# A third late q chunk, Wp in the freed accumulation banks, a scheduler with small waits and perturbed passes, and 12 warm matmuls instead of 16, in a two-pair linear-attention and FFN kernel

## The chip, the cores and the metric

The kernel runs on one core of one Trainium2 chip. Times are device microseconds of a run; the number quoted for a kernel is the median of its runs. A run's *span* is the time from its first to its last instruction. Every run has the granted TensorE clock in its records (1.0 is full speed).

## The reference, cut to what matters

```python
# x: (1, 2048, 512) bf16; wqkv: (512, 1536); wo: (512, 512); w1: (512, 1376); w2: (1376, 512)
phi = lambda t: jnp.where(t > 0, t + 1, jnp.exp(t)) + 1e-6
def A(x):                      # linear attention, 32 heads of 16
    q, k, v = heads(x @ wqkv)
    kv  = einsum("bhsd,bhse->bhde", phi(k), v)       # a sum over all 2048 rows
    z   = einsum("bhsd->bhd", phi(k))
    num = einsum("bhqd,bhde->bhqe", phi(q), kv)
    den = einsum("bhqd,bhd->bhq", phi(q), z) + 1e-6
    return merge(num / den) @ wo
def B(x): return relu(x @ w1) @ w2
x = x + A(layernorm(x));  x = x + B(layernorm(x))
x = x + A(layernorm(x));  x = x + B(layernorm(x))
```

No output of an attention layer can be computed before the sums `kv` and `z` over all rows are done. That is the *barrier* of this document; there are two.

## The kernel before

The kernel is a graph of operations, each with an engine, a modelled duration, and what it reads and writes. A list scheduler in the kernel's own Python orders the operations of each engine when the kernel is built; the order is then fixed, and each engine runs its list in order, waiting on semaphores. The 2048 rows are 16 tiles, or 4 chunks of 4 tiles. `k`, `gacc` (accumulation for kv, in four PSUM banks `GB` that stay taken), `z`, `q`, `den`/`denb` (denominator and its reciprocal, spread over the heads), `u` (scaling of q), `wp` (kv times wo), `wo` (output projection), `h` and `ffo` (the two halves of the FFN) are its steps.

```python
# scheduler, forward pass, for each engine e:
            st0 = min(c[0] for c in cands)
            lim = st0 + SLACK[e]                     # SLACK is 0 everywhere before
            st, o = min((c for c in cands if c[0] <= lim), key=lambda c: (-c[1].prio, c[1].idx))
...
# each q or k group: two evictions on ScalarE, two operations on VectorE
g.add(ACT, ... activation(dst_ap, psv[:, b, :], Identity, bias=1.0 + 1e-6) ..., name="_lin")
g.add(ACT, ... activation(escr[:, s, :], psv[:, b, :], Exp) ...,            name="_exp")
g.add(DVE, ... tensor_scalar(emscr[:, s, :], escr[:, s, :], 1.0, 1e-6, min, add) ..., name="_em")
g.add(DVE, ... tensor_tensor(dst_ap, dst_ap, emscr[:, s, :], max) ...,      name="_phi")
...
def bar():                                           # the barrier, in program order
    late = list(range(max(0, NCH - Q_LATE), NCH))    # Q_LATE = 2: chunks 2 and 3
    for i in range(NT - LAG, NT): a_g_acc(i, GB)
    ... a_z_acc ...; a_z_final(zb); a_g_evac(GB)
    for t in late[:LATE_A]: a_q_proj(t, late=True)
    a_kv()
    for t in range(DEN_PRE): a_den(t, GB)
    for t in late[LATE_A:]: a_q_proj(t, late=True)
    a_wp()
...
def a_wp():
    for j in range(4):
        b = alloc_bank()                             # any free PSUM bank
        mm_group(... KVT[:, j, :], wo[:, j, :] ... -> bank b); evac_flex(Wp[:, j, :] <- bank b)
...
# denominator of chunk t: four matmuls, then ScalarE Ln and Exp(-), VectorE rhi and rsp,
# four matmuls into the GB banks, four VectorE multiplications "u"
```

A `q` chunk that isn't late is computed in the projection phase, between the k groups. A layer norm's output reaches TensorE by DMA transposes, two tiles each (the first chunk's by TensorE).

## Time and profile before

| | before |
|---|---|
| time, median of the first 3 runs | 295.24 us |
| span of the profiled run | 293.0 us |
| TensorE busy, by the page | 282.9 us (97%) |
| VectorE, ScalarE busy | 164.0 us (56%), 171.8 us (59%) |
| first useful TensorE instruction | 7.18 us |
| last matmul starts | 290.04 us |

The page's part 1, engine: busy us (share of the span) and instructions:

```profile
PE 282.9 (97%) x1470; PEld 129.3 (44%) x1491; DVE 164.0 (56%) x485; ACT 171.8 (59%) x349; POOL 20.7 (7%) x32
```

97% doesn't mean that 3% is all there is to win or to lose: the Trainium skill says ("Perfetto Trace Analysis", Per-engine timelines) that a matmul's end is computed, not observed, and this trace gives matmuls of 379 ns mean that start 216 ns apart. So I count what TensorE *lost* from start times: the step from one matmul's start to the next, less what that shape takes in an unbroken stream (128x512: 0.216 us; 128x256: 0.109; 128x128: 0.056; one column: 0.026; a group of four tiled denominator matmuls: 0.318). The page has 1491 weight loads and only 1470 matmuls: some matmul records are missing, so a surplus of just one more 0.216 us is taken for a missing record. (Where the clock is at half, this count is blind: each matmul then looks like a missing record.) Sums of these steps:

| stretch | lost before |
|---|---|
| start: until the first useful instruction, and steps up to 36 us | 7.18 + 1.39 = 8.57 us |
| first barrier and the FFN beside it, 36 to 86 us | 2.89 us |
| 86 to 155 us | 0.19 us |
| second barrier, 174 to 228 us | 2.99 us |

About 0.6 us of the first barrier's sum are six steps of 0.1 us around the tiled groups. The rest sits at three steps around the Wp matmuls (0.52, 0.24, 0.26 us) and one that looks like 1.50 us. The view of TensorE's waits for 36 to 86 us (line waited for: us, times, longest), then the timeline (start us, us, engine, line, op, out<-in, count, idle before):

```profile
PE ps L573 <- DVE emscr L557: 1.4, 1, 1.4
PE ps L573 <- DVE Wp L652: 0.4, 1, 0.4
```

```profile
58.54 2.61 SPq L522 DMA_TRANSPOSE Tb<-xn  x2
...
59.53 2.47 DVE L720 TENSOR_TENSOR big<-big,ps 128x512 bf16<-128x512 bf16 x4
...
60.47 0.40 PE L573 MATMUL ps<-big,Zc 128*32 128x512 bf16 x4
...
62.06 2.27 PEld L573 LDWEIGHTS ps<-Wp,big 128*128 128x128 bf16 x12 [1.49 <-DVE big L720]
62.29 2.54 PE L573 MATMUL ps<-Wp,big 128*128 128x512 bf16 x11 [1.43 <-DVE emscr L557]
```

At 60.8 us TensorE has run out of late q groups. The next in its list is chunk 1's output projection (`ps<-Wp,big`), which needs the four scalings (`big<-big,ps`) that end at 62.0; its weight loads name them as what they waited for. Chunk 0's transposes were issued at 58.54 and land at 63.82 and 64.60, so no FFN matmul is ready either. And in the view of windows (busy us and count of PE, PEld, DVE, ACT, POOL; clock; DMA) VectorE and ScalarE have no room here:

```profile
54.00:64.00 10.00, 8.57 (x45) 3.55 (x44) 10.00 (x31) 9.67 (x23) 0.00 (x0) 1.00 0.54 54
```

### The profile page before, as it was taken

How to read it: one execution, taken by the hardware profiler on the slowest of the kernel's cores; microseconds unless marked ns; L12 is line 12 of the kernel's file. 1: busy time of each engine (PE TensorE's matmuls, PEld its weight loads, DVE VectorE, ACT ScalarE, POOL GpSimd, SP SyncE). 2: the span in 40 equal slices, each digit the busy share in tenths (PEclk: the TensorE clock that was granted, in tenths of full speed). 3: DMA queues.
4: the chain of work that ended last, by engine and by line, in shares of the span. 5: the costliest groups of instructions: out<-in, count | busy, mean ns of one | idle time of the engine just before them, and what ended most of it. 6: DMA issues, size and time to landing. Idle time of an engine off the chain costs nothing.

```text
span 293.0 us, 4025 instructions
## 1 busy us (share of the span) xinstructions
PE 282.9 (97%) x1470; PEld 129.3 (44%) x1491; DVE 164.0 (56%) x485; ACT 171.8 (59%) x349; POOL 20.7 (7%) x32
## 2 busy tenths in 40 slices
PE   7999999989999999999999999998999999999996
PEld 2444445434444444444444444533444444444443
DVE  5998637996349551480326474599832955130233
ACT  1888757997664583597623486599766407317000
POOL 4213000002001110010001100000100011000000
PEclk9999999999999999999999999999999999999999
DMA  6945930073003070030000340004610424001022
GB/s 224 346 78 104 303 122 2 0 75 61 10 2 72 0 143 2 1 72 0 3 0 0 72 74 0 2 0 73 39 36 0 34 71 112 0 11 63 0 72 74
DMA packets 40163, 17.23 MB, mean 59 GB/s; under 512 B 31984, under 2 KB 39632, under 8 KB 40144
## 3 DMA queue, kind: packets, MB, share of 16 engines
q1 hardware_dynamic: 40144, 16.98, 26.7%
q8 instruction: 12, 0.20, 0.3%
q14 instruction: 7, 0.06, 0.1%
HBM read 7.01 MB, written 2.10 MB: 31 GB/s over the span
## 4 chain that ended last, share of the span: by engine, by line
PE 83%; DVE 11%; DMA 3%; issue 1%; SPq 0%
PE ps L573 83%; DVE big L720 3%; DMA xin<-in_A_x_dram 2%; DVE xres L586 2%; DMA Tb<-xn 1%; DVE big L559 1%; DVE Wp L652 1%; DVE bst L483 1%; DVE emscr L557 1%; DVE xn L593 1%; DVE rsp L714 1%; DVE rhi L713 0%; DVE xn L515 0%; DVE nmf L589 0%; DVE xin L760 0%
## 5 line engine op out<-in xcount | busy, mean ns | idle before, releaser
L573 PE MATMUL ps<-Tb,w 128*128 128x512 bf16 (+1 forms) x352 | 78.0, 379 | 0.0
L573 PE MATMUL ps<-w,big 128*128 128x512 bf16 (+3 forms) x355 | 76.4, 372 | 0.4
L741 ACT ACTIVATE big<-ps 128x512 bf16<-128x512 f32 (+1 forms) x81 | 48.2, 596 | 29.4 <-PE ps L573 28.9
L580 ACT ACTIVATE sqscr<-xres 128x512 bf16<-128x512 f32 x48 | 30.3, 635 | 42.7 <-DVE xres L617 27.9
L573 PEld LDWEIGHTS ps<-w,big 128*128 128x128 bf16 (+1 forms) x363 | 35.4, 98 | 40.8
L573 PEld LDWEIGHTS ps<-Tb,w 128*128 128x128 bf16 (+1 forms) x352 | 34.9, 100 | 40.9 <-issue 0.9
L555 ACT ACTIVATE escr<-ps 128x512 bf16<-128x512 f32 x64 | 38.4, 613 | 9.7 <-PE ps L573 9.7
L553 ACT ACTIVATE big<-ps 128x512 bf16<-128x512 f32 x64 | 38.3, 613 | 3.0 <-PE ps L573 3.0
L613 DVE SCALAR_TENSOR_TENSOR xin<-ps,rstdf,xres 128x512 bf16<-128x512 f32 x15 | 11.3, 750 | 38.5 <-PE ps L573 38.5
L573 PE MATMUL ps<-wqkv,Tb 128*128 128x512 bf16 x125 | 31.4, 379 | 0.3
L573 PE MATMUL ps<-Wp,big 128*128 128x512 bf16 x124 | 28.7, 379 | 3.0 <-DVE emscr L557 2.9
L573 PE MATMUL ps<-big,xn 128*128 128x512 bf16 x124 | 31.3, 379 | 0.2
L573 PE MATMUL ps<-Tb,wqkv 128*128 128x512 bf16 x128 | 30.5, 380 | 0.1
L557 DVE TENSOR_SCALAR emscr<-escr 128x512 bf16<-128x512 bf16 x64 | 17.8, 290 | 21.7 <-ACT escr L555 21.2
L559 DVE TENSOR_TENSOR big<-big,emscr 128x512 bf16<-128x512 bf16 x64 | 26.0, 422 | 3.9 <-ACT big L553 3.5
L617 DVE SCALAR_TENSOR_TENSOR xres<-ps,rstdf,xres 128x512 f32<-128x512 f32 x16 | 12.0, 751 | 24.8 <-PE ps L573 24.8
L720 DVE TENSOR_TENSOR big<-big,ps 128x512 bf16<-128x512 bf16 x32 | 20.1, 681 | 7.9 <-PE ps L573 7.9
L573 PEld LDWEIGHTS ps<-Wp,big 128*128 128x128 bf16 x128 | 12.2, 98 | 17.6 <-DVE big L720 3.0
L573 PEld LDWEIGHTS ps<-big,xn 128*128 128x128 bf16 x128 | 12.5, 98 | 15.1 <-DVE big L559 0.2
L573 PEld LDWEIGHTS ps<-wqkv,Tb 128*128 128x128 bf16 x128 | 12.2, 98 | 15.2 <-DMA Tb<-xn 0.6
L573 PEld LDWEIGHTS ps<-Tb,wqkv 128*128 128x128 bf16 x128 | 11.7, 98 | 15.3 <-issue 1.8
L606 POOL TENSOR_TENSOR rstdf<-varf,nhalf 128x4 f32<-128x4 f32 x8 | 8.1, 1007 | 144.6 <-DVE varf L604 144.6
(76 smaller groups left out, 180.7 us busy)
## 6 DMA issues: line engine op xcount, KB each, us to landing
wqkv<-in_A_wqkv_dram SPq DMA_DIRECT2D x3, 512.0 KB, 6.9
xin<-in_A_x_dram SPq DMA_DIRECT2D x3, 512.0 KB, 7.9
out_dram<-xin SPq DMA_DIRECT2D x3, 512.0 KB, 2.9
w<-in_B_w_dram SPq DMA_DIRECT2D x1, 1376.0 KB, 6.3
w<-in_B_w_dram SPq DMA_DIRECT2D x1, 1280.0 KB, 9.8
wo<-in_A_wo_dram SPq DMA_DIRECT2D x1, 512.0 KB, 8.6
Tb<-xn SPq DMA_TRANSPOSE x30, 3.2
xin<-in_A_x_dram SPq DMA_DIRECT2D x1, 384.0 KB, 3.3
```

Source lines behind the costliest of these rows:

```text
L553: g.add(ACT, lambda e: e.activation(dst_ap, psv[:, b, :], ACTF.Identity, bias=1.0 + 1e-6, scale=1.0), [("ps", b)], [dst_key], C_ACT_PSUM, ...
L555: g.add(ACT, lambda e: e.activation(escr[:, s, :], psv[:, b, :], ACTF.Exp), [("ps", b)], [("escr", s)], C_ACT_EXP, name=name + "_exp")
L557: g.add(DVE, lambda e: e.tensor_scalar(emscr[:, s, :], escr[:, s, :], 1.0, 1e-6, ALU.min, ALU.add), [("escr", s)], [("emscr", s)], C_DVE_B ...
L559: g.add(DVE, lambda e: e.tensor_tensor(dst_ap, dst_ap, emscr[:, s, :], ALU.max), [dst_key, ("emscr", s)], [dst_key], 340.0, name=name + "_ ...
L573: last = e.matmul(o, l, r, start=st, stop=sp, skip_group_check=skip)
L580: g.add(ACT, lambda e: e.activation(sqscr[:, q, :], xres[:, i, :], ACTF.Square, accum_out=dst[:, i:i + 1]), [("xres", i)], [("sqscr", q), ...
L586: g.add(DVE, lambda e: e.scalar_tensor_tensor(xres[:, i, :], psv[:, b, :], 0.0, src, ALU.add, ALU.add, accum_out=s1f[:, i:i + 1]), [("ps", ...
L606: g.add(POOL, lambda e: e.tensor_tensor(rstdf[:, sl], varf[:, sl], nhalf[:, 0:4], ALU.pow), [("varf", t), ("nhalf",)], [("rstdf", t)], C_P ...
L613: g.add(DVE, lambda e: e.scalar_tensor_tensor(xin[:, i, :], psv[:, b, :], rstdf[:, i:i + 1], xres[:, i, :], ALU.mult, ALU.add), rd, [("xin ...
L617: g.add(DVE, lambda e: e.scalar_tensor_tensor(xres[:, i, :], psv[:, b, :], rstdf[:, i:i + 1], xres[:, i, :], ALU.mult, ALU.add, accum_out= ...
L720: g.add(DVE, lambda e, j=j: e.tensor_tensor(unit_ap(us[j]), unit_ap(us[j]), psv[:, GB[j], :], ALU.mult), [("big", us[j]), ("ps", GB[j])], ...
L741: g.add_flex([(ACT, lambda e, M=M, b=b, u=u: e.activation(unit_ap(u, M), psv[0:M, b, :], ACTF.Relu), C_ACT_PSUM), (DVE, lambda e, M=M, b=b ...
```

## The change

Its intent is to give TensorE other work across the barrier, to take bank waits out of it, and to let the scheduler pass over an operation that is ready for a more urgent one that comes within a small wait. The core of the diff:

```diff
-SLACK = {PE: 0.0, ACT: 0.0, DVE: 0.0, POOL: 0.0, SP: 0.0}
+SLACK = {PE: 60.0, ACT: 100.0, DVE: 150.0, POOL: 0.0, SP: 0.0}
 # modelled costs: C_DVE_STT 615 -> 630, C_DVE_NORM_BF 325 -> 330, transposes 470 + 740 a tile ->
 # 1270 + 550 a tile, DMA latency 1500 -> 1600, one-column matmul 30 -> 26
@@ def _list_schedule
-    for _ in range(iters):                       # 6 passes, best total kept
+    for k in range(iters):                       # 12 passes, best score kept
         _backward(ops, succ, rank)
+        ...
+        sigma = rng.choice((0.0, 0.0, 200.0, 600.0, 2000.0)) if k >= 4 else 0.0
         for o in ops:
-            rank[o.idx] = o.t_start
+            rank[o.idx] = src[4][o.idx][3] + rng.gauss(0.0, sigma)
+    for _ in range(search):                      # search is 0
+        ...
-def build_kernel(..., Q_LATE=2, ..., WARM=16, ..., ITERS=6):
+def build_kernel(..., Q_LATE=3, ..., WARM=12, ..., WP_GB=True, ..., ITERS=12, SEARCH=0, ...):
@@
-        def a_wp():
+        def a_wp(GB):
             for j in range(4):
-                b = alloc_bank()
+                b = GB[j] if WP_GB else alloc_bank()
```

Cut: options that stay off (row sums on GpSimd, statistics on ScalarE, a load from ScalarE's queue), and the activation table load, which moves behind leading DMA issues of ScalarE's queue (there are none).

More of the change, by code (lines that the diff above doesn't have):

```diff
@@ L1 @@
 import contextlib
-import math
+import random
 import concourse.bass as bass
@@ L24 @@
 C_DVE_PSUM = 600.0
-C_DVE_STT = 615.0
+C_DVE_STT = 630.0
+C_DVE_STTP = 690.0
 C_DVE_BF4X = 205.0
@@ L28 @@
 C_DVE_BNST = 595.0
-C_DVE_NORM_BF = 325.0
+C_DVE_NORM_BF = 330.0
 C_POOL_POW = 1000.0
@@ L38 @@
 C_SP_ISSUE = 470.0
+C_SP_TR = 1270.0
+C_MMN1 = 26.0
 TAIL = {PE: 70.0, ACT: 230.0, DVE: 80.0, POOL: 300.0, SP: 0.0}
 SYNC_LAT = 40.0
-SLACK = {PE: 0.0, ACT: 0.0, DVE: 0.0, POOL: 0.0, SP: 0.0}
+SLACK = {PE: 60.0, ACT: 100.0, DVE: 150.0, POOL: 0.0, SP: 0.0}
 class _Op:
     __slots__ = ("eng", "emit", "reads", "writes", "dur", "lat", "sdeps", "odeps", "idx",
-                 "seq", "dma", "name", "t_start", "t_done", "t_ready", "issued", "prio", "alts")
+                 "seq", "dma", "name", "t_start", "t_done", "t_ready", "issued", "prio", "alts", "force", "cls")
     def __init__(self, eng, emit, reads, writes, dur, lat, dma, name):
@@ L59, in __init__ @@
         self.alts = None
+        self.force = None
+        self.cls = name.rstrip("0123456789_")
         self.seq = None
@@ L218, in _forward @@
                 st = max(t, fa)
-                if o.alts:
+                if o.force is not None:
+                    if o.force != e:
+                        continue
+                elif o.alts:
                     mine = [d for (x, _, d) in o.alts if x == e][0]
@@ L263, in _forward @@
         if o.dma:
-            dma_free = max(st + 1500.0, dma_free) + o.lat
+            dma_free = max(st + 1600.0, dma_free) + o.lat
             o.t_done = dma_free + 500.0
@@ L280, in _forward, with _list_schedule, score, run @@
     return total, order, vbank, bank_after, snap
-def _list_schedule(ops, tile_ops, vbank, fixed_sp, iters=6, nbanks=8):
+def _list_schedule(ops, tile_ops, vbank, fixed_sp, iters=6, search=0, nbanks=8):
     succ = _succs(ops)
+    npe = float(sum(1 for o in ops if o.eng == PE))
+    def score(res):
+        return res[0] + 0.05 * sum(v[3] for v in res[4].values() if v[0] == PE) / npe
+    def run():
+        for o in ops:
+            o.prio = base[o.idx] + bias[o.idx]
+        try:
+            return _forward(ops, succ, tile_ops, nbanks, fixed_sp)
+        except RuntimeError:
+            return None
+    rng = random.Random(7)
     rank = {o.idx: float(o.idx) for o in ops}
-    best = None
-    for _ in range(iters):
+    bias = [0.0] * len(ops)
+    best = best_base = None
+    for k in range(iters):
         _backward(ops, succ, rank)
-        res = _forward(ops, succ, tile_ops, nbanks, fixed_sp)
-        if best is None or res[0] < best[0]:
+        base = [o.prio for o in ops]
+        res = run()
+        if res is not None and (best is None or score(res) < score(best)):
+            best, best_base = res, base
+        src = res if res is not None and k % 8 != 7 else best
+        sigma = rng.choice((0.0, 0.0, 200.0, 600.0, 2000.0)) if k >= 4 else 0.0
+        for o in ops:
+            rank[o.idx] = src[4][o.idx][3] + rng.gauss(0.0, sigma)
+    base = best_base
+    for _ in range(search):
+        old_bias = list(bias)
+        snap = best[4]
+        c = rng.choice(ops)
+        t0 = snap[c.idx][3]
+        w = rng.choice((2000.0, 6000.0, 15000.0))
+        sd = rng.choice((100.0, 400.0, 1500.0))
+        for o in ops:
+            if abs(snap[o.idx][3] - t0) <= w:
+                bias[o.idx] += rng.gauss(0.0, sd)
+        res = run()
+        if res is not None and score(res) <= score(best):
             best = res
-        for o in ops:
-            rank[o.idx] = o.t_start
+        else:
+            bias = old_bias
     total, order, vb, bank_after, snap = best
@@ L306, in _list_schedule, with build_kernel @@
     return order, total
-def build_kernel(nc, A_x, A_wqkv, A_wo, B_w1, B_w2, out, n_layers_pairs=2, Q_LATE=2, O_PE_CHUNKS=3, PHI_PATH=3,
-                 KV_LAG=2, INTERLEAVE=True, WARM=16, SPLIT_CHUNKS=1, TAIL_SPLIT=True,
+def build_kernel(nc, A_x, A_wqkv, A_wo, B_w1, B_w2, out, n_layers_pairs=2, Q_LATE=3, O_PE_CHUNKS=3, PHI_PATH=3,
+                 KV_LAG=2, INTERLEAVE=True, WARM=12, SPLIT_CHUNKS=1, TAIL_SPLIT=True,
                  PHI_K=3, PHI_QE=3, PHI_QL=3, LAST_HALVES=True, ZH_FIRST=True, P2_TIGHT=False,
-                 FIRST_PE_CHUNKS=1, TGK=2, TGF=2, WO_LAG=1, DEN_PRE=1, LATE_A=1, ITERS=6):
+                 FIRST_PE_CHUNKS=1, TGK=2, TGF=2, FT_PE=0, WP_GB=True, WO_LAG=1, DEN_PRE=1, LATE_A=1, ITERS=12, SEARCH=0, ZP=0, WK_ACT=False, ACT_STATS=()):
     S = A_x.shape[1]
@@ L375, in build_kernel @@
         Zc = sb("Zc", [128, 4, 32], BF16)
+        zacc = sb("zacc", [128, 512], F32)
+        zhl = sb("zhl", [128, 2, 512], BF16)
         GT = sb("GT", [128, 4, 512], BF16)
@@ L404, in build_kernel, with dma @@
         scr_state = {"e": 0, "sq": 0, "ln": 0}
-        def dma(emit, reads, writes, xfer_ns, name):
+        def dma(emit, reads, writes, xfer_ns, name, eng=SP, issue=C_SP_ISSUE):
             sem = es.enter_context(nc.semaphore("dsem%d" % len(dma_sems)))
@@ L411, in _emit @@
                 return emit(eng).then_inc(sem, 16)
-            op = g.add(SP, _emit, reads, writes, dur=C_SP_ISSUE, lat=xfer_ns, dma=True, name=name)
+            op = g.add(eng, _emit, reads, writes, dur=issue, lat=xfer_ns, dma=True, name=name)
             op.seq = sem
@@ L439, in build_kernel @@
         ld_x(0, 1)
-        dma(lambda e: e.dma_start(wqkv[:, :, D:2 * D], wq_v[:, :, D:2 * D]), [], [("wk",)], 1600.0, "ld_wk")
+        dma(lambda e: e.dma_start(wqkv[:, :, D:2 * D], wq_v[:, :, D:2 * D]), [], [("wk",)], 1600.0, "ld_wk", eng=ACT if WK_ACT else SP)
         for t in range(1, NCH):
@@ L446, in build_kernel @@
         dma(lambda e: e.dma_start(wo[:], A_wo.rearrange("(c p) n -> p c n", p=128)), [], [("wo",)], 1600.0, "ld_wo")
-        early_loads = list(g.ops)
+        early_loads = [o for o in g.ops if o.eng == SP]
         nfull = NFC - 1 if FLAST < 128 else NFC
@@ L453, in build_kernel @@
             dma(lambda e: e.dma_start(w2[0:FLAST, NFC - 1, :], B_w2[nfull * 128:DFF, :]), [], [("w2b",)], 600.0, "ld_w2b")
-        late_loads = g.ops[len(early_loads):]
+        late_loads = [o for o in g.ops if o.eng == SP][len(early_loads):]
         W2KEYS = [("w2a",), ("w2b",)] if FLAST < 128 else [("w2a",)]
@@ L523, in tr_dma @@
                                                 xn[:, lo:hi, :].rearrange("p i d -> p (i d)")),
-                [("xn", i) for i in range(lo, hi)], [("T", i) for i in range(lo, hi)], 740.0 * (hi - lo), "tr%d" % lo)
+                [("xn", i) for i in range(lo, hi)], [("T", i) for i in range(lo, hi)], 550.0 * (hi - lo), "tr%d" % lo, issue=C_SP_TR)
         def tr_chunk(t, grain):
@@ L626, in a_k_proj @@
             phi_evac(b, pk_tile(i), ("big", pk_unit(i)), "k%d" % i, path=PHI_K)
+            if 0 < i < 4 * ZP:
+                prev = pk_tile(0) if i == 1 else zacc[:, :]
+                pkey = ("big", pk_unit(0)) if i == 1 else ("zacc",)
+                g.add(POOL, lambda e: e.tensor_tensor(zacc[:, :], prev, pk_tile(i), ALU.add),
+                      [("big", pk_unit(i)), pkey], [("zacc",)], C_POOL_TT, name="zp%d" % i)
+                if i == 4 * ZP - 1:
+                    g.add(POOL, lambda e: e.tensor_copy(zhl[:, 0, :], zacc[:, :]), [("zacc",)], [("zhl", 0)], C_POOL_CP, name="zhi")
+                    g.add(POOL, lambda e: e.tensor_tensor(zhl[:, 1, :], zacc[:, :], zhl[:, 0, :], ALU.subtract),
+                          [("zacc",), ("zhl", 0)], [("zhl", 1)], C_POOL_TT, name="zlo")
         def a_g_acc(i, GB):
@@ L632, in a_g_acc, with a_z_acc, src @@
                      [("big", u), ("xn", i)], [("ps", b) for b in GB], 4 * C_MM512, "gacc%d" % i)
-        def a_z_acc(lo, hi, zb):
-            def mk():
-                mms = []
-                for i in range(lo, hi):
-                    u = pk_unit(i)
-                    for j in range(4):
-                        mms.append((psv[:, zb, j:j + 1], big[:, u * 512 + 128 * j:u * 512 + 128 * j + 128], ones[:, 0:1],
-                                    i == 0 and j == 0, i == NT - 1, True))
-                return mms
-            mm_group(mk, [("big", pk_unit(i)) for i in range(lo, hi)] + [("ones",)], [("ps", zb)], (hi - lo) * 4 * C_MMTINY, "z%d" % lo)
+        def a_z_acc(lo, hi, zb, first):
+            def src(i, j):
+                if i < 0:
+                    return zhl[:, i + 2, 128 * j:128 * j + 128]
+                u = pk_unit(i)
+                return big[:, u * 512 + 128 * j:u * 512 + 128 * j + 128]
+            def mk():
+                return [(psv[:, zb, j:j + 1], src(i, j), ones[:, 0:1], first and i == lo and j == 0, i == NT - 1, True)
+                        for i in range(lo, hi) for j in range(4)]
+            mm_group(mk, [("zhl", i + 2) if i < 0 else ("big", pk_unit(i)) for i in range(lo, hi)] + [("ones",)], [("ps", zb)],
+                     (hi - lo) * 4 * C_MMN1, "z%d" % lo)
         def a_z_final(zb):
@@ L798, in ln_tile_first @@
         def ln_tile_first(i):
-            ln_stats_first(i)
             c = slice(i, i + 1)
+            if i in ACT_STATS:
+                g.add(ACT, lambda e: e.activation(sqscr[:, 0, :], xin[:, i, :], ACTF.Identity, accum_out=s1[:, c]),
+                      [("xin", i)], [("sqscr", 0), ("s1", i)], C_ACT_SQ, name="sm%d" % i)
+                g.add(ACT, lambda e: e.activation(sqscr[:, 1, :], xin[:, i, :], ACTF.Square, accum_out=s2[:, c]),
+                      [("xin", i)], [("sqscr", 1), ("s2", i)], C_ACT_SQ, name="sq%d" % i)
+                g.add(DVE, lambda e: e.tensor_scalar(mv[:, i, 0:1], s1[:, c], INV_D, None, ALU.mult),
+                      [("s1", i)], [("mean", i)], C_DVE_SMALL, name="mean%d" % i)
+                g.add(DVE, lambda e: e.scalar_tensor_tensor(nm2[:, c], mv[:, i, 0:1], -1.0, mv[:, i, 0:1], ALU.mult, ALU.mult),
+                      [("mean", i)], [("nm2", i)], C_DVE_SMALL, name="nm2_%d" % i)
+                g.add(DVE, lambda e: e.scalar_tensor_tensor(mv[:, i, 1:2], s2[:, c], INV_D, nm2[:, c], ALU.mult, ALU.add),
+                      [("s2", i), ("nm2", i)], [("var", i)], C_DVE_SMALL, name="var%d" % i)
+            else:
+                ln_stats_first(i)
             g.add(DVE, lambda e: e.tensor_scalar(veps[:, c], mv[:, i, 1:2], 0.0, EPS, ALU.max, ALU.add),
@@ L864, in bar @@
                     zb = alloc_bank()
-                    for k in range(NCH):
-                        a_z_acc(4 * k, 4 * k + 4, zb)
+                    if ZP:
+                        a_z_acc(-2, 0, zb, True)
+                    for k in range(ZP, NCH):
+                        a_z_acc(4 * k, 4 * k + 4, zb, k == 0)
                     a_z_final(zb)
@@ L875, in bar @@
                         a_q_proj(t, late=True)
-                    a_wp()
+                    a_wp(GB)
                 def p2(t):
@@ L883, in p2 @@
                             a_wo(i, first_layer)
-                        tr_chunk(t - WO_LAG, TGF)
+                        if t - WO_LAG < FT_PE:
+                            for i in range(4 * (t - WO_LAG), 4 * (t - WO_LAG) + 4):
+                                transpose_pe(i)
+                        else:
+                            tr_chunk(t - WO_LAG, TGF)
                         ln_ffn(t - WO_LAG)
@@ L924, in build_kernel @@
             cur = nxt
-        order, total = _list_schedule(g.ops, g.tile_ops, vbank, early_loads + first_tr + late_loads, ITERS)
+        order, total = _list_schedule(g.ops, g.tile_ops, vbank, early_loads + first_tr + late_loads, ITERS, SEARCH)
         for e in (PE, ACT, DVE, POOL):
-            for k, o in enumerate(order[e]):
+            for k, o in enumerate([o for o in order[e] if not o.dma]):
                 o.seq = k + 1
@@ L958, in emit_engine @@
         def emit_engine(e, handle):
+            lead = True
             for o in order[e]:
+                if e == ACT and lead and not o.dma:
+                    lead = False
+                    handle.preload_act_table_set("natural_log_exp_and_others")
                 for d in waits[o.idx]:
@@ L978, in _ @@
             def _(s):
-                s.preload_act_table_set("natural_log_exp_and_others")
                 emit_engine(ACT, s)
```

## The prediction

> **What bounds the kernel now.** The page gives TensorE 282.9 of 293.0 us busy (97%). The Trainium skill ("Perfetto Trace Analysis", Per-engine timelines) says that matmul ends are estimated, so I go by start-to-start times. In the timeline a 128x512 matmul starts 0.216 us after the one before it; the skill's 215.7 ns ("TensorE: Matmul & The Clock Gate", Part 1) agrees. Lone 0.43 us steps I take for missing records. TensorE loses time only here:
> - Start: first useful instruction at 7.18 us; steps too long by 0.5, 0.1 and 0.3 us up to 9.5 us, and 0.26 us at 18.5 us, where the first DMA-transposed tile lands (18.89).
> - Each attention barrier (44-63 and 184-203 us): 0.5, 0.25, 0.25 (around the Wp matmuls, waiting for Wp evictions, for a bank or for the reciprocal) and 1.6 us (60.8 to 62.3, output projection of chunk 1 waiting for VectorE): 2.6 us each.
> - Tail: last matmul starts 3.0 us before the end.
>
> No useful matmul is removed, so the ceiling is about 5.2 us at the barriers plus 1.5 to 2 at the start.
>
> **What the change does.**
> 1. Third late q chunk: 16 matmuls (4 groups of 0.86 us, 3.5 us) move from the projection phase into each barrier, as filler for the hole. They bring 8 ScalarE evictions of 0.60 us (4.8 us) and VectorE 4 x (0.29+0.42) = 2.8 us. The windows view has VectorE 9.00 and ScalarE 8.67 busy of the 9 us of 54-63: filler loads the saturated engines. But 36-48 has over 5 us free on each, and the accumulation now ends 3.5 us earlier.
> 2. Wp in the accumulation banks: no wait for a free bank (0.5+0.25 us), but the Wp matmuls must wait until the first scaling by the reciprocal has read those banks. They move from 47.6-48.9 to about 51-53 us. The reciprocal chain gets ahead of the Wp evictions on VectorE (about 1 us), which pays for it; the first output projection stays near where it was.
> 3. Small waits (60/100/150 ns) and perturbed passes: urgent small VectorE operations no longer lose to 0.6 us ones. The first tile's bias waits from 4.61 (power done) to 6.53; chunk 1's from 13.17 to 13.71. I expect the first transpose at 5.5-6 us and chunk 1's transpose issued 0.8 us before 14.87. The load of x chunk 1 (lands 8.19, on the chain of waits) doesn't move, so the start gains about 0.8 us, not 1.9.
> 4. 12 warm matmuls end 0.86 us earlier, near 5.2 us. The first 8 take 0.43 us, the rest 0.216, so the clock is up by then. Alone worth nothing: the first transpose waits for xn.
> 5. Less filler before the second attention's last chunk (165-169 us): chunk 0's q groups (3.5 us) and chunk 2's work (6.9 us) still cover until chunk 3's transpose lands (173.4). No new hole.
>
> **Sum.** Start -0.8; each barrier regains about 1.8 of 2.6 us, -3.6 in all; tail unchanged: 295.2 - 4.4 = 290.8 us. Range 288.8 to 293.4. Faster by over 2% (below 289.3): 0.2; within 2%: 0.79; slower: 0.01.
>
> **What would show it.** TensorE's 1.8 us step in each barrier shrinks under 0.8; the steps at the Wp matmuls vanish, these now after the first scaling; the first DMA transpose is issued before 14.5 us; useful matmuls unchanged; span about 288.6.
>
> **What would make it wrong.** Filler saturates ScalarE (12 q groups need 14.6 us), q groups wait for banks, and the barriers gain under 1 us. Or better order closes all holes: about 287.5. Or the static order, made for modelled times, stalls where a load lands later than modelled.

## The result

| | before | after |
|---|---|---|
| time, median of 4 runs each | 295.22 us | 290.79 us |
| range | 295.13 to 295.36 | 290.42 to 291.80 |
| ratio, 95% interval | | 0.9855 (0.983 to 0.988) |
| span of the profiled run | 293.0 us | 289.0 us |
| last matmul starts | 290.04 us | 286.01 us |
| lost at the start | 8.57 us | 6.67 + 2.08 = 8.75 us |
| lost in the first barrier | 2.89 us | 0.89 us |
| lost in the second barrier | 2.99 us | 0.90 us |

The kernel is 1.45% faster: "same" at the 2% threshold, as predicted, and the predicted 290.8 us is met. The middle of the sum isn't met as well. The barriers gained 2.00 and 2.09 us where 1.8 each was predicted, and the start lost 0.18 us where a gain of 0.8 was predicted. (With about 0.1 us between the barriers, these add up to the 4.03 us that the last matmul moved. The medians are 4.43 us apart: the profiled run of "before" took 294.85 us, 0.37 us less than its median, that of "after" 290.85 us.)

The page's engine line, the same window, and the timeline of the first barrier after the change. In the view of TensorE's waits for 36 to 86 us no line is left.

```profile
PE 281.1 (97%) x1465; PEld 128.7 (45%) x1487; DVE 166.7 (58%) x479; ACT 176.3 (61%) x355; POOL 19.8 (7%) x32
```

```profile
54.00:64.00 10.00, 9.95 (x51) 4.15 (x50) 9.74 (x28) 9.80 (x21) 0.00 (x0) 1.00 0.28 54
```

```profile
54.67 2.99 SPq L566 DMA_TRANSPOSE Tb<-xn  x2
...
58.51 0.40 PE L617 MATMUL ps<-rsp,esel 32*128 32x512 bf16 x4
...
58.84 1.04 PE L617 MATMUL ps<-Tb,wqkv 128*128 128x512 bf16 x4
...
58.96 2.48 DVE L775 TENSOR_TENSOR big<-big,ps 128x512 bf16<-128x512 bf16 x4 [0.16 <-PE ps L617]
...
59.72 2.75 PE L617 MATMUL ps<-Tb,w 128*128 128x512 bf16 x12
...
62.52 3.40 PE L617 MATMUL ps<-Wp,big 128*128 128x512 bf16 x15
```

Busy TensorE time is still 97% of a shorter span: that number shows nothing of the change. The scalings take 2.48 us as before and VectorE and ScalarE are as full as before. But there are q groups until 59.5 us, and then three FFN groups (`ps<-Tb,w`) come before chunk 1's output projection, since chunk 0's transposes are issued at 54.67 and land at 57.76 and 59.49. The wait is gone because TensorE has something else to do, not because what it waited for is faster.

### The profile page after: what moved, and what is told of

It reads as the page before. It is cut to its first block, busy times and chain, and to the rows that moved or that the text cites. A ratio compares the mean times of both kernels' runs of the same rounds, so it can differ in the third digit from the quotient of the medians. Undisturbed runs are those within 1.5% of the kernel's fastest.

```text
span 289.0 us, 4009 instructions
## 1 busy us (share of the span) xinstructions
PE 281.1 (97%) x1465; PEld 128.7 (45%) x1487; DVE 166.7 (58%) x479; ACT 176.3 (61%) x355; POOL 19.8 (7%) x32
## 4 chain that ended last, share of the span: by engine, by line
PE 89%; ACT 4%; DVE 2%; DMA 2%; issue 1%; SPq 0%
PE ps L617 89%; DMA xin<-in_A_x_dram 2%; ACT escr L599 2%; ACT big L597 2%; DVE bst L527 1%; ACT big L796 1%; DVE xn L559 0%; ACT lden L766 0%; DVE emscr L601 0%; DVE xin L815 0%; SPq L484 0%; DVE big L603 0%; SPq L479 0%; SPq L481 0%; DVE mv L528 0%
## 5 line engine op out<-in xcount | busy, mean ns | idle before, releaser
L617 PE MATMUL ps<-w,big 128*128 128x512 bf16 (+2 forms) x356 | 76.4, 373 | 0.4
L796 ACT ACTIVATE big<-ps 128x512 bf16<-128x512 f32 (+1 forms) x78 | 46.2, 599 | 27.2 <-PE ps L617 26.8
L599 ACT ACTIVATE escr<-ps 128x512 bf16<-128x512 f32 x64 | 38.5, 620 | 10.7 <-PE ps L617 10.1
L597 ACT ACTIVATE big<-ps 128x512 bf16<-128x512 f32 x64 | 38.5, 620 | 0.7 <-PE ps L617 0.6
```

The lines of the kernel that those rows point to most:

```text
L597: g.add(ACT, lambda e: e.activation(dst_ap, psv[:, b, :], ACTF.Identity, bias=1.0 + 1e-6, scale=1.0), [("ps", b)], [dst_key], C_ACT_PSUM, ...
L599: g.add(ACT, lambda e: e.activation(escr[:, s, :], psv[:, b, :], ACTF.Exp), [("ps", b)], [("escr", s)], C_ACT_EXP, name=name + "_exp")
L617: last = e.matmul(o, l, r, start=st, stop=sp, skip_group_check=skip)
L796: g.add_flex([(ACT, lambda e, M=M, b=b, u=u: e.activation(unit_ap(u, M), psv[0:M, b, :], ACTF.Relu), C_ACT_PSUM), (DVE, lambda e, M=M, b=b ...
```

## The experiments

The theory after the result was that the third late q chunk is the filler that closes the hole; rivals were the freed banks and the new scheduler. The experiments took 12 kernels in three lots, the first on another chip than the other two; each ratio is to runs of "before" in the same rounds. (In a_q2 to a_w16f, one of the seven runs of "before", 297.19 us, has a clock of 0.994, which makes ratios 0.1% too low.) In the edits, "before" and "after" are the two kernels.

One thing needed no run. The kept pass of "after" is the second of 12, and noise sets in with the fifth. With `sigma = 0.0` the compiled program is the same, byte for byte. **The randomised passes do nothing in this kernel**, and the search that the change adds is switched off. In b_sched and a_q2 below the noise does change the compiled program, so their orders are in part a matter of chance.

### Each part alone on the kernel before

b_q3:
```diff
-    Q_LATE=2
+    Q_LATE=3
```

> The kernel before with only the third late q chunk (old scheduler, Wp in ordinary banks, 16 warm matmuls). Theory (filler): the chunk alone closes the 1.5 us hole of each barrier, so each barrier loses about 1 us or a little more instead of 3.1, last matmul about 4 us earlier: 291.0 to 291.8. Rival (the new scheduler did it): at most 1 us of gain, 294.2 or more.

Measured: 292.86 us, ratio 0.9922 (0.9903 to 0.9942). The barriers lose 1.91 and 2.02 us: 1.0 us less than before each, about half of the change's gain there. Both ranges were missed: filler alone does a large part and not all. What is left in each barrier, besides 0.33 and 0.19 us around the Wp matmuls and the steps of 0.1 us, is a new step of 0.78 us, not at the output projection but between the second and third FFN group.

b_gb:
```diff
-                b = alloc_bank()      # in a_wp
+                b = GB[j]
```

> The kernel before with only Wp in the accumulation banks (old scheduler, two late chunks). Filler theory: removes the 0.5+0.25 us steps at the Wp matmuls at best, but the 1.5 us hole stays or grows since the Wp matmuls now wait for the first scaling: 294.5 to 296.5. Rival (freed banks did it): 292.5 or less.

Measured: 296.26 us, ratio 1.0033 (1.0001 to 1.0064); barriers 3.21 and 3.30 us. The steps at the Wp matmuls go, but a step of 0.53 us comes before the first output projection, and the hole before chunk 1's projection grows from 1.29 to 2.09 us. Alone the banks cost 0.3 us a barrier. In the time that is hardly clear of noise: one of the four runs (297.55 us) has a clock of 0.994, and the other three have a median of 296.01 us.

b_q3gb is both edits.

> The kernel before with the third late chunk and Wp in the accumulation banks, old scheduler. Filler theory: like b_q3 within 0.7 us. Rival (the banks matter once the filler is there): at least 1 us faster than b_q3.

Measured: 292.85 us, ratio 0.9918; barriers 2.22 and 2.27 us, about 0.3 us each more than b_q3; the time is the same. Its hole is before the first FFN group, waiting for chunk 0's transpose (issued at 56.78 and 58.12, landed at 60.07 and 61.31):

```profile
PE ps L573 <- DMA Tb<-xn: 1.2, 1, 1.2
```

b_sched is the changed kernel with three knobs turned back:
```diff
-    Q_LATE=3, WARM=12, WP_GB=True
+    Q_LATE=2, WARM=16, WP_GB=False
```

> The changed kernel with two late chunks, Wp in ordinary banks and 16 warm matmuls, so the new scheduler, its slack and its costs alone. Filler theory: with 8 late groups instead of 12 TensorE still runs out of work in each barrier, 1.5 us or more lost in each: 293 to 295. Rival (scheduler): barriers lose about 0.9 us each, 290.5 to 291.5.

Measured: 294.97 us, ratio 0.9998 (0.9959 to 1.0037); barriers 2.56 and 2.27 us. So the scheduler alone shows no gain in the time, as the filler theory said, though the barriers lose 0.3 and 0.7 us less. One of its four runs (the profiled one, 297.04 us) shows a mean clock of 0.994, more on that below; the other three have a median of 294.7 us, so a gain of 0.6 us isn't excluded.

### Each part taken out of the changed kernel

a_q2:
```diff
-    Q_LATE=3
+    Q_LATE=2
```

> The changed kernel with two late q chunks again, all else as changed. The third late chunk alone took 1.2 us out of each barrier. If it is the necessary part, taking it away brings each barrier back to a loss of 2.2 us or more: 293.3 to 295. If the banks and the scheduler do most of it, below 292.

Measured: 295.76 us, ratio 1.0003; barriers 2.86 and 2.50 us, with a 2.16 us hole before chunk 1's projection. The barriers came out as expected; the time is above the range named. Three of the four runs have the clock at 0.993 or 0.994; the fourth took 294.54 us, inside the range and 0.6 us below "before". Without the third late chunk the change is worth about half a microsecond.

a_nogb:
```diff
-    WP_GB=True
+    WP_GB=False
```

> The changed kernel with Wp in ordinary banks, all else as changed. If the freed banks matter (bank waits while filler runs), each barrier loses 0.7 us more than the changed kernel's 0.9 us, 292.2 or more. If they don't: within 0.6 us of the changed kernel, 290.2 to 291.4.

Measured: 293.67 us, ratio 0.9935; barriers 1.83 and 1.84 us. The steps: 0.56 us where TensorE waits for the reciprocal, which on VectorE stands behind a Wp eviction (eviction at 44.98, `rhi` at 45.59 us), and 0.62 us again between the second and third FFN group. Two of four runs had the clock at 0.994; the other two took 292.80 and 293.99 us.

a_slack0:
```diff
-SLACK = {PE: 60.0, ACT: 100.0, DVE: 150.0, ...}
+SLACK = {PE: 0.0, ACT: 0.0, DVE: 0.0, ...}
```

> The changed kernel with the three slacks at 0 (a ready operation is never passed over for a more urgent one that comes 60 to 150 ns later). If the small waits are what brings chunk 0's transposes early in the barrier, the issue of the first comes 0.7 us or more later after the first output projection (3.6 us in the changed kernel, 4.6 before), a hole comes back before the first FFN matmul, and the time is 291.8 or more. If the costs do it: within 0.6 us of the changed kernel.

Measured: 293.41 us, ratio 0.9931; barriers 1.79 and 1.80 us. The first transpose was issued 4.18 us after the first output projection (51.41 to 55.59), 0.58 us later than in the changed kernel: a little under what was named. But that was not the wait: TensorE had started on the FFN at 60.54 us, and its step of 0.95 us is once more before the third FFN group:

```profile
PE ps L617 <- ACT big L597: 0.8, 1, 0.8
```

### Why three partly changed kernels wait before the third FFN group

b_q3, a_nogb and a_slack0 have one order in common that "after" doesn't have: chunk 2's denominator matmuls come before the first FFN group, in "after" behind the seventh. A new theory: the reciprocal's Ln and Exp then stand in ScalarE's list among the q evictions, and the FFN groups wait for the banks that these evictions free. The Trainium skill says that ScalarE's queue is strict first-in-first-out ("TensorE: Matmul & The Clock Gate", Part 1), so an operation that nobody needs yet holds up all behind it. Two kernels test it, each with one ordering edge and no other edit.

after_inv:
```diff
+        for d, o in zip([o for o in g.ops if o.name == "den2"], [o for o in g.ops if o.name == "h0_0"]):
+            o.odeps.append(d)
         order, total = _list_schedule(...)
```

> The changed kernel with one ordering edge: chunk 2's denominator matmuls must come before the first FFN group of TensorE (as every partly changed kernel had it), in both barriers. Everything up to the first output projection stays as it is. Theory (ScalarE's queue): the two reciprocal activations of chunk 2 (0.69 and 0.62 us) then stand among the q evictions, the FFN groups wait for a PSUM bank and a hole of 0.6 to 0.9 us comes back in each barrier: 292.0 to 292.8. Rival (the holes of the partly changed kernels come from something else): no more than 0.3 us a barrier, 291.4 or less.

Measured: 292.91 us, ratio 0.9928 (0.9910 to 0.9946), median span 290.2 us against 288.95: just above the range named. Each barrier loses 1.57 us, 0.68 and 0.67 more than "after". The timeline of after_inv shows it:

```profile
59.17 0.40 PE L617 MATMUL ps<-big,Zc 128*32 128x512 bf16 x4
...
59.62 0.69 ACT L764 ACTIVATE lden<-ps,eps 128x512 f32<-128x512 f32 x1
...
59.83 1.90 PE L617 MATMUL ps<-Tb,w 128*128 128x512 bf16 x8
...
60.21 0.59 ACT L599 ACTIVATE escr<-ps 128x512 bf16<-128x512 f32 x1
60.68 0.63 ACT L766 ACTIVATE lden<-lden 128x512 f32<-128x512 f32 x1
61.20 0.60 ACT L599 ACTIVATE escr<-ps 128x512 bf16<-128x512 f32 x1
61.68 1.09 ACT L597 ACTIVATE big<-ps 128x512 bf16<-128x512 f32 x2
...
62.34 1.04 PE L617 MATMUL ps<-Tb,w 128*128 128x512 bf16 x4 [0.61 <-ACT big L597]
```

Ln (L764) and Exp (L766) are in front of the q evictions (L599, L597), and the third FFN group starts when the first eviction of the pair begun at 61.68 us has freed its bank. Nothing needs this reciprocal before chunk 2's projection, far behind.

b_q3_e4 does the reverse to the *old* scheduler:
```diff
 # b_q3, and:
+        for d, o in zip([o for o in g.ops if o.name == "h0_4"], [o for o in g.ops if o.name == "den2"]):
+            o.odeps.append(d)
```

> The kernel before with the third late chunk (old scheduler, Wp in ordinary banks) and one ordering edge: chunk 2's denominator matmuls come after the fifth FFN group. Theory (ScalarE's queue): the 0.78 us step of b_q3 before the third FFN group goes from both barriers, each loses 1.3 us or less, 291.0 to 291.8, so filler and this order alone give most of the change's gain without its scheduler or its banks. Rival: within 0.5 us of b_q3 (292.86).

Measured: the step of 0.78 us is gone from both barriers; they lose 1.20 and 1.21 us instead of 1.91 and 2.02, inside the expectation. The time missed it: 292.72 us (ratio 0.9916), median span 290.95 us against 291.05 of b_q3. By the time alone it is the rival's range that was met. In the profiled run, which was its fastest (span 290.1), the start lost 9.27 us, 0.66 more than in b_q3, since the edge gave the old scheduler another order there too; that takes back 0.66 of the 1.52 us that the barriers gave. Its other three runs have spans of 290.8 to 291.7 us and were not profiled, so why they are longer is open. The edge thus settles the mechanism in the barrier, not that one edge could replace the new scheduler.

### The start

a_w16f emits four more warm matmuls and keeps the order:
```diff
-                for k in range(WARM):
+                for k in range(WARM + 4):
```

> The changed kernel's schedule to the instruction, with 16 warm matmuls emitted in place of 12. The four more end near 6.1 us, the first transpose waits for xn until 6.67 us: no difference, 290.4 to 291.2. Rival (the warm matmuls were in the way): 0.5 us or more slower.

Measured: 290.89 us, ratio 0.9848 (changed kernel: 0.9855), median span 289.05 us against 288.95. No difference, as expected. In its profiled run the clock rose late (at 5.97 us), the warm matmuls did hold the first transpose up until 7.02 us, and later steps were shorter by as much (lost at the start: 8.69 us).

The predicted gain at the start didn't come. Chunk 1's first transpose was indeed issued at 14.18 instead of 14.87 us and landed at 17.49 instead of 18.89, but TensorE had fallen behind with chunk 0 and only reached it at 18.11 us. VectorE in "after", 7.2 to 10 us:

```profile
7.86 0.15 DVE L872 SCALAR_TENSOR_TENSOR nbias<-mv,rstd 128x1 f32<-128x1 f32 x1
8.43 0.70 DVE L527 BATCH_NORM_STATS2 bst<-xin 128x6 f32<-128x512 bf16 x1 [0.42 <-DMA xin<-in_A_x_dram]
9.04 0.14 DVE L872 SCALAR_TENSOR_TENSOR nbias<-mv,rstd 128x1 f32<-128x1 f32 x1
```

The last bias of chunk 0 (9.04) stands behind the statistics of chunk 1 (8.43), which wait for their load. The scheduler's model has this load at 6.97 us, which is 7.75 us when both count from the first DMA issue (0.78 us in the trace); it landed at 8.41. a_x corrects that one constant:
```diff
-        dma(... [("wk",)], 1600.0, "ld_wk", ...)
+        dma(... [("wk",)], 2200.0, "ld_wk", ...)
```

> The changed kernel whose scheduler is told that x chunk 1 lands 0.6 us later, as the trace shows (8.4 us); one constant, barriers stay as they are. Theory A (the start is limited by chunk 0's own normalisation, whose last bias stood behind chunk 1's statistics that waited for their load): TensorE's loss up to 36 us falls from 8.75 us to 8.2 or less, 290.0 to 290.4. Theory B (the start is limited by VectorE, full until chunk 2's transposes): the loss moves to the wait for chunk 2's transpose near 25 us, total within 0.2 us of the changed kernel, 290.6 to 291.0.

Measured: the first useful instruction comes at 7.51 us, and TensorE's waits after it are 0.30 us at full clock and, counted by hand, 0.16 us at half clock: 8.0 us in all, about 0.7 less than in "after", as theory A had it; the barriers lose 0.89 us each as they should. But the time missed theory A's range in every run: it was 291.75 us, ratio 0.9889, slower than the changed kernel: five of its six runs have a mean clock of 0.994. The one without it took 290.61 us (span 288.6). In the profiled run the clock went to half from 8.11 to 11.52 us (windows, the column before the last two is the clock):

```profile
4.70:8.11 3.41, 1.47 (x11) 0.57 (x10) 3.30 (x15) 0.17 (x1) 1.60 (x4) 1.00 1.03 323
8.11:11.52 3.41, 3.41 (x15) 1.54 (x16) 3.33 (x11) 2.92 (x6) 0.41 (x1) 0.50 1.06 363
```

3.41 us at half clock cost up to 1.7 us, and 1.5 us is what its last matmul (286.83 us) is later than "after" less 0.7 us would be. The 12 warm matmuls end near 5.7 us and the first transpose is at 7.51 us; the period with this gap in it ends at 8.11 us, and there the clock fell.

a_xs was a try for a faster kernel: a_x with the change's own search turned on.
```diff
-    SEARCH=0
+    SEARCH=2000
```

> a_x with 2000 steps of the change's own random search, which the change leaves at 0: a try for a faster kernel. The search finds little that a trace would call lost (the barriers' loss above the tiled groups' own steps is nearly 0), so 289.9 to 290.8; if the orders it finds rest on modelled times too closely, slower than a_x by 0.5 us or more.

Measured: 290.92 us, ratio 0.9856 (0.9836 to 0.9877), a hair over the range named and not slower than a_x; median span 289.2 us. Barriers 0.97 and 0.95 us, start 8.85 us, one of five runs with the low clock. It is level with the changed kernel. No kernel here beats that one clearly. Whether a_x with 16 warm matmuls would keep its 0.7 us wasn't run.

## Why the prediction was right or wrong

- **What bounds the kernel: right.** TensorE's lost time was where the prediction had it. All of the gain came from the barriers, whose ceiling was named as 5.2 us; 4.1 of it was won, and 0.4 of it were the two unrecorded matmuls, counted as waiting.
- **Step 1, filler: right in kind, a little too small.** Predicted: each barrier regains about 1.8 us. It was 2.0 and 2.1. The third chunk is the necessary part (a_q2: about half a microsecond in all without it) and gives 1.0 us a barrier alone (b_q3). The prediction feared that filler would saturate ScalarE and q groups would wait for banks; this does happen, for FFN groups, but only where chunk 2's reciprocal is put among the evictions (0.7 us, after_inv). It didn't foresee that this order would be the difference.
- **Step 2, banks: right that they pay for themselves.** The Wp matmuls came after the start of the scaling (47.04; Wp at 48.6 to 49.9 us) and no longer wait. The stated 51 to 53 us forgot that the whole barrier begins earlier. Alone the banks cost 0.3 us a barrier (b_gb), with the filler they don't change the time under the old scheduler (b_q3gb), and in the changed kernel they take away a 0.56 us wait for the reciprocal (a_nogb).
- **Step 3, small waits: wrong in place.** They were booked as 0.8 us at the start. There they gave nothing (8.57 to 8.75 us lost): chunk 1's transpose did go out 0.69 us earlier, but the same order put chunk 0's last normalisation behind a load. In the barrier, not named, turning them off costs 0.9 us each (a_slack0), with the step before the third FFN group, which after_inv ties to the order of chunk 2's reciprocal, as its largest part. "Perturbed passes" were named as acting at all; the compiled program shows that they don't.
- **Step 4, warm matmuls: right for this kernel, reason incomplete.** Going back to 16 changed nothing (a_w16f). But "the clock is up by then" isn't enough: it can fall again, as in a_x and a_q2, and with 16 warm matmuls in b_sched.
- **Step 5, no new hole before the second attention's last chunk: right.** TensorE loses nothing there beyond one step that looks like a missing record (0.22 us at 158.9 us).
- **The sum: right in total, in part by luck.** 290.8 predicted, 290.79 measured, but the start fell short by 1.0 us and the barriers gained 0.5 us more than predicted. The rest is the 0.37 us by which the profiled run of "before", from which the prediction was worked out, was shorter than its kernel's median.

Open: how the scheduler's gain divides between its waits and its corrected costs (a_slack0 shows the waits, nothing shows the costs alone), whether the same order is behind the steps of a_nogb and a_slack0 (it was tested on "after" and b_q3 alone), and why b_q3_e4's unprofiled runs are longer than its profiled one.

## What to carry to other kernels

Where a reduction over all rows forces a wait, keep back independent matmuls for it, and count what their evictions cost on engines that are already full there: the filler is worth its whole price only if nothing that isn't needed yet stands in front of those evictions in an in-order queue. A part that shows no gain alone, like the banks here, can still take away a wait that only the other parts expose, so test it both ways, added to the old and taken from the new. Where a trace lacks records, pair loads with matmuls before a wait's length is believed. Before crediting a search or its noise, compare the programs it makes: here they were the same.

## What the Trainium skill lacked or had wrong

- "TensorE: Matmul & The Clock Gate", Part 1, has the clock fall to half after at least one idle window of about 3.4 us, and its section "Why this matters for your kernels" warns of idle gaps over about 3 us. The 3.41 us period agrees (a_x: 4.70, 8.11, 11.52 us), but no window was idle (the page's section on PSUM-queue cycling does tell of a clock that swings with short pauses, but gives no limit): a_x fell after a period with TensorE 1.47 us of 3.41 busy, a_q2 after 1.28, b_sched after 1.34; periods with 1.68 ("after"), 1.69 (a_nogb) and 1.77 us (after_inv) did not. In a_x the longest wait was 1.8 us. In these fourteen traces the limit lies between 1.47 and 1.68 us busy in one period, and the changed kernel is close to it. (TensorE's busy time counts computed matmul ends.) The lines of a_q2, b_sched and "after", in this order:

```profile
4.41:7.82 3.41, 1.28 (x8) 0.44 (x7) 3.23 (x12) 0.54 (x1) 1.43 (x3) 1.00 1.05 352
```

```profile
7.51:10.93 3.42, 1.34 (x14) 0.88 (x15) 1.81 (x7) 1.78 (x4) 0.55 (x1) 1.00 1.02 325
```

```profile
4.13:7.54 3.41, 1.68 (x10) 0.62 (x8) 3.07 (x13) 0.44 (x1) 1.58 (x3) 1.00 1.02 327
```

- The same page, Part 2, Back-to-back issue gap, gives about 131 ns as the sustained spacing of matmuls with N=512 in a real kernel and calls 216 ns the isolated figure. Here they start 216 ns apart in unbroken streams of dozens, each with its own weight load.
- None of the pages I used says that matmul records can be missing: the profile of "after" has 1465 matmuls and 1487 weight loads. (The pages on notification queues say in general that a full queue can drop records, but don't tie this to a profile's matmuls.) Steps of 0.43 us in a stream of 0.216 us look like waits until this is known, and a record missing at the end of a true wait makes the wait look 0.22 us longer (62.07 instead of 62.29 us in "before").
